# Input rows dealt to partitions in runs, u transposed in 64-row pieces, and held output work given buffers of its own

## The chip, the cores and the metric

One core of a Trainium2 chip runs the kernel. The metric is the device time of one execution in microseconds (us), the median of several runs. Five engines work side by side, each in the order in which its instructions were written: TensorE (PE, matrix multiplication), VectorE (DVE), ScalarE (ACT), GpSimd (POOL) and SyncE (SP). In this kernel SP issues the plain transfers and the transposing transfers, and POOL issues those that change the type on the way from float32 to bfloat16 ("casts"). An instruction that waits for a semaphore holds up everything behind it on its engine.

## The reference: what is computed

There are 8 batches of 3136 rows and 256 columns. The first part is an attention without softmax, the second a gate with a long convolution along the rows, written with FFTs.

```python
scores = (1 / S) * z @ z.T                   # z: S x 64, S = 3136
out    = (np.maximum(scores, 0) ** 2) @ v    # v: S x 256
x      = u * out
proj   = x @ w_proj                          # 256 x 768: x1, x2, x3
x2_conv = irfft(rfft(x2, axis=1) * rfft(filter_fft, axis=0), n=S, axis=1)
y      = (x1 * x2_conv * x3) @ w_out
```

Only the order of the rows inside a batch is free: sums over rows do not depend on it, and the result must stand in the original order in memory.

## The kernel before: how the work is laid out

S is split as 3136 = 64 x 49. A row has the number 49 n1 + n2, with n1 below 64 and n2 below 49. The convolution is a two-step Fourier transform: first over n1 (64 points, `dft1`, one matmul with the table `T1` for two values of n2 at once), then over n2 (49 points, with the tables `S2`). The way back uses `TZ` and `T4`. On chip a tile of 128 partitions holds two values of n2, 64 partitions each; NT = 25 such tiles make a batch, the last one half full. Before the change tile t holds n2 = 2t on the lower half and 2t + 1 on the upper half, so that in the on-chip order the rows stand by n2, and within it by n1.

For each batch b:

- POOL casts z, v and u to bfloat16 (`cast_z`, `load_rows`, `cast_u`). z and u go to scratch in memory, `z16d` and `u16d`, already in the on-chip order: a write of 64 numbers of z, or of 256 numbers of u (512 B), at a time. v goes to SBUF.
- SP reads them back transposed: `ldz` for z (one transfer, `zT`), `load_uT` for u (one transfer for each of seven chunks of 384 to 512 rows, `uT`).
- For each chunk of columns: scores into PSUM (`score_mm`, L1066), ReLU on ACT (L1104), square on ACT or DVE (L1110, L1112) into one of 7 buffers `A`, then v times A (`weigh`, L1135). DVE multiplies with `uT` (L1177) and gives `xT`.
- `add_proj` multiplies xT with w_proj: two parts become the gates (L775, L787, L793), one goes through `dft1` (L821, L653) and is put into scratch memory (`put`, L660).
- `add_spectrum`, when all seven chunks of a batch are in: 8 groups. Each loads its part (`load_spec`, L683), does the second transform (L866), the product with the filter's spectrum (L888), the transform back (L910), and puts the result (`gs_t`, two buffers, L933).
- `add_end`: 7 groups. Each loads (`load_c`, L694), transforms over n1 (L964), multiplies with the gates (L971), multiplies with w_out (L1002), evicts into an output buffer (`ost_t`, two buffers) and stores (L1029).

The order of all instructions is not written by hand. Each piece is a `Task` with a cost on each engine that may do it, the tasks that it depends on and the buffers that it takes. `Plan.go` simulates the engines with these costs when the kernel is built and emits each engine's instructions in the order in which it starts them. PE takes scores (kind S) and v times A (W) first, and fills in the rest (FA, FB, FZ) between them; so the spectrum and the end of batch b run while batch b + 1 does its scores. The planner counts 1.3 us of SP for a `load_uT` and 1.3 for a store.

The last batches are treated apart. Of batch 6 only the first group of `add_end` runs as usual; the other six are held back for the time when batch 7 has no more scores (kind FZ). They depend on `q_`, the last square of batch 7, and load into the buffers `A`, which are free from then on. Their output uses the two `ost_t` buffers. Batch 7's own output uses `R` and `zs` buffers.

At the start POOL issues, in this order: v in two parts with the first part of u between them, two more parts of u, the filter, then the two weight matrices `wp` and `wo` (L346 to L395). The tables are built from `iota` on POOL, DVE arithmetic and a sine on ACT; `percol` (L470 to L479) computes per-partition constants, among them n2 for the row of S2.

Transfers wait on semaphores of which SP and POOL have eight each, taken in turn: a transfer is issued once the one eight before it on the same queue has landed.

Of the kernel before, what the change touches and what calls it, by code (L numbers as in the profile page):

```python
# [11 lines left out]
P = 128  # L12
# [218 lines left out]
def kernel(  # L231
# [27 lines left out]
    z16d = [dram.tile([S, P], BF16, name=f"z16d{i}") for i in range(2)]  # L259
# [81 lines left out]
    def rows_n2(x):  # L341
        return x.rearrange("(n2 n1) d -> n1 n2 d", n1=N1)

    def cast_z(b):
        for k in range(2):
            nc.gpsimd.dma_start(out=rows_n2(z16d[b % 2][:, ds(k * dqk, dqk)]), in_=rows_n1(z[b]))  # L346

    def cast_u(b, lo=0, hi=N2):
        nc.gpsimd.dma_start(out=rows_n2(u16d[b % 2][:, :])[:, lo:hi, :], in_=rows_n1(u[b])[:, lo:hi, :])
# [4 lines left out]
    def load_rows(t, src, t0=0, t1=NT):  # L354
        r = rows_n1(src)
        for j in range(2):
            e = min(t1, (N2 + 1 - j) // 2)
            nc.gpsimd.dma_start(
                out=t[ds(j * N1, N1), t0:e, :], in_=r[:, 2 * t0 + j : 2 * (e - 1) + j + 1 : 2, :]
            )  # L360
# [15 lines left out]
    for i, (t0, t1) in enumerate(((0, 16), (16, NT))):  # L376
        for j in range(2):
            e = min(t1, (N2 + 1 - j) // 2)
            nc.sync.dma_start(
                out=zf[i][ds(j * N1, N1), 0 : e - t0, :], in_=zr[:, 2 * t0 + j : 2 * (e - 1) + j + 1 : 2, :]  # L380
            )
# [5 lines left out]
    cast_u(0, 0, 8)  # L387
    load_rows(v16[0], v[0], 6, NT)
    cast_u(0, 8, 22)
    cast_u(0, 22, N2)  # L390
    load_rows(filt, moe_filter_fft)
    wp16 = const.tile([P, 2, 3 * D], BF16, name="wp16")
    nc.gpsimd.dma_start(out=wp16[:], in_=moe_w_proj.rearrange("(t p) n -> p t n", p=P))
    wo16 = const.tile([P, 2, D], BF16, name="wo16")
# [75 lines left out]
    def percol():  # L470
# [3 lines left out]
        nc.vector.scalar_tensor_tensor(cp, n2p, -2.0, pf, ALU.mult, ALU.add)  # L474
        nc.vector.tensor_scalar(ph0, cp, -float(QUART), float(QUART), ALU.mult, ALU.add)
# [471 lines left out]
    def add_end(b, lasts, gtasks, tg, kind="FB", src=l_p, dsts=(o_p,), late=0):  # L947
        for t0, nt in tg:
# [7 lines left out]
            for dh in range(2):  # L956
# [12 lines left out]
                def ev(dh=dh, t0=t0, w=w, box=box, yb=yb):  # L969
# [4 lines left out]
                    kind, mm, c_pe(*[rows] * nt), [ld, t4_done, *firsts, *(e for _, e in gtasks)],  # L974
# [50 lines left out]
            def store(t0=t0, nt=nt, rows=rows, ob=ob):  # L1025
                r = rows_n1(out[b])
                for j in range(rows // N1):
                    a = 2 * t0 + j
                    nc.sync.dma_start(out=r[:, a : a + 2 * nt - 1 : 2, :], in_=ob["o"][ds(j * N1, N1), 0:nt, :])  # L1029

            s_ = on("SP", store, 1.3, oe, prio=1, moves=0.45 * nt)
            s_.frees.append((o0, 1))


    uT = {}
# [222 lines left out]
```

## Time and profile before

| | us |
|---|---|
| median of 3 runs (lowest to highest) | 1161.12 (1160.87 to 1162.87) |
| the profiled execution | 1163.63 |
| its span, first to last instruction | 1161.9 |
| PE busy | 1112.9 (96%) |
| ACT busy | 1049.2 (90%) |
| DVE busy | 929.6 (80%) |
| POOL busy | 67.5 (6%) |
| chain that ended last: PE, DMA, DVE, ACT | 87%, 5%, 3%, 2% |

How to read what follows. Times in the profile are in us from the start of the span unless a row says ns. A row of a timeline has the start, the length, the engine, the source line and operation, what it writes and reads, and how many instructions were merged. `SPq` is SP's queue: the length of a DMA row is the time for which SP was busy issuing it, not the time until its data landed. A group's row ends with the engine's idle time before its instructions and what ended it (the releaser). A row of waits reads: engine and tile, line, what it waited for, us in total, times, longest. A row of stretches has the stretch, its length, the busy time of PE, PE's weight loads, DVE, ACT and POOL (number of instructions in brackets), the granted share of TensorE's clock, the DMA share and GB/s. Line numbers are those of the kernel before.

### The profile page before, as it was taken

Reading aid. Unit: us, or ns where it says so; the run is one execution under the profiler, and the core shown is the slowest. Engines: PE = TensorE matmul, PEld = TensorE weight load, DVE = VectorE, ACT = ScalarE, POOL = GpSimd, SP = SyncE. Lnnn points to the kernel's source line nnn. Section 1 sums busy time; section 2 is a strip of 40 time slices with the busy share of each in tenths; the row PEclk is TensorE's granted clock in tenths of the full one; section 3 lists DMA queues with packets and bytes.
Section 4 is the critical chain, followed back from the end, with each engine's and each line's share of the span. In section 5 each row is a group of like instructions: output and inputs, shape, how many; then the busy total and the mean of one; then the engine's idle time right before and its main releaser. Section 6 shows DMA issues by size and latency. Waiting matters only on the chain.

```text
span 1161.9 us, 18975 instructions
## 1 busy us (share of the span) xinstructions
PE 1112.9 (96%) x6903; PEld 545.8 (47%) x6903; DVE 929.6 (80%) x1358; ACT 1049.2 (90%) x1464; POOL 67.5 (6%) x80
## 2 busy tenths in 40 slices
PE   5899999999999999899999999999999999999974
PEld 2344445544455444345445543555445454454463
DVE  5898889887798788689788877888778876887673
ACT  5899999999999999798999999998999999999862
POOL 4110002000110002000020001100020000000000
PEclk9999999999999999899999999999999999999987
DMA  9973719443791439934296534944399342312266
GB/s 175 115 115 76 130 56 197 86 121 98 109 197 50 102 78 188 147 91 108 62 186 120 125 89 86 208 97 113 85 118 187 99 111 52 96 49 59 63 191 187
DMA packets 274222, 134.24 MB, mean 116 GB/s; under 512 B 128576, under 2 KB 260800, under 8 KB 274128
## 3 DMA queue, kind: packets, MB, share of 16 engines
q1 hardware_dynamic: 175664, 99.58, 36.2%
q0 software_dynamic: 98464, 33.44, 25.5%
q8 instruction: 54, 0.88, 0.3%
q14 instruction: 40, 0.33, 0.1%
HBM read 94.98 MB, written 71.45 MB: 143 GB/s over the span
## 4 chain that ended last, share of the span: by engine, by line
PE 87%; DMA 5%; DVE 3%; ACT 2%; issue 1%; POOL 1%; SPq 0%; ACTq 0%; DVEq 0%; POOLq 0%
PE ps_o_t L1135 45%; PE ps_s_t L1066 13%; PE ps_m_t L910 4%; PE ps_m_t L821 4%; PE ps_m_t L787 4%; PE ps_m_t L775 4%; PE ps_m_t L1002 3%; DMA wp<-in_moe_w_proj_dram 3%; PE ps_m_t L866 2%; PE ps_m_t L653 2%; PE ps_m_t L964 2%; DMA spec<-gs_t 1%; PE ps_s_t L1068 1%; ACT R_t L1104 1%; PE ps_m_t L735 1%
## 5 line engine op out<-in xcount | busy, mean ns | idle before, releaser
L1135 PE MATMUL ps_o_t<-A_t,v_t 128*128 128x512 bf16 (+4 forms) x2800 | 652.2, 354 | 0.6 <-DVE A_t L1112 0.2
L1104 ACT ACTIVATE R_t<-ps_s_t 128x1024 f32<-128x1024 f32 (+5 forms) x728 | 616.6, 890 | 28.1 <-PE ps_s_t L1066 22.0
L1112 DVE TENSOR_TENSOR A_t<-R_t 128x768 bf16<-128x768 f32 (+3 forms) x411 | 432.8, 1061 | 73.7 <-ACT R_t L1104 50.9
L1135 PEld LDWEIGHTS <-v_t 128*128 128x128 bf16 (+1 forms) x2800 | 255.1, 98 | 242.3 <-issue 84.1
L1110 ACT ACTIVATE A_t<-R_t 128x1024 bf16<-128x1024 f32 (+4 forms) x317 | 288.7, 916 | 21.9 <-PE ps_o_t L1135 17.4
L1066 PE MATMUL ps_s_t<-zT_t 64*128 64x512 bf16 (+2 forms) x1344 | 194.4, 357 | 2.9 <-ACT R_t L1104 2.9
L1066 PEld LDWEIGHTS <-zT_t 64*128 64x128 bf16 x1344 | 42.9, 94 | 124.2 <-issue 121.8
L793 DVE TENSOR_TENSOR gate_t<-ps_m_t,x_t 128x512 bf16<-128x512 f32 (+2 forms) x111 | 66.3, 619 | 22.8 <-PE ps_m_t L787 15.9
L329 DVE CAST x_t<-ps_m_t 128x512 bf16<-128x512 f32 (+4 forms) x112 | 67.4, 613 | 20.5 <-PE ps_m_t L821 15.4
L1177 DVE SCALAR_TENSOR_TENSOR xT_t<-ps_o_t,uT_t 128x512 bf16<-128x512 f32 (+2 forms) x112 | 69.0, 618 | 14.0 <-PE ps_o_t L1135 13.6
L888 DVE TENSOR_TENSOR zs_t<-xs_t,H 98x2048 bf16<-98x2048 bf16 x60 | 73.0, 1217 | 0.7 <-ACT xs_t L325 0.2
L971 DVE TENSOR_TENSOR yT_t<-ps_m_t,gate_t 128x128 bf16<-128x128 f32 (+4 forms) x162 | 62.1, 423 | 13.1 <-PE ps_m_t L964 12.7
L910 PE MATMUL ps_m_t<-zs_t,TZ 98*98 98x256 bf16 x460 | 70.3, 276 | 0.5 <-ACT gs_t L325 0.5
L325 ACT ACTIVATE x_t<-ps_m_t 128x512 bf16<-128x512 f32 (+4 forms) x118 | 61.6, 540 | 9.7 <-PE ps_m_t L775 5.3
L910 PEld LDWEIGHTS <-TZ 98*98 98x98 bf16 x512 | 57.6, 126 | 21.8 <-issue 12.0
L821 PE MATMUL ps_m_t<-wp,xT_t 128*128 128x256 bf16 (+1 forms) x400 | 60.1, 274 | 0.6 <-DVE xT_t L1177 0.5
L775 PE MATMUL ps_m_t<-xT_t,wp 128*128 128x512 bf16 (+2 forms) x220 | 56.7, 362 | 3.0 <-DMA wp<-in_moe_w_proj_dram 3.0
L329 DVE CAST s_t<-ps_m_t 128x512 bf16<-128x512 f32 (+2 forms) x70 | 41.2, 592 | 22.4 <-PE ps_m_t L653 21.7
L787 PE MATMUL ps_m_t<-xT_t,wp 128*128 128x512 bf16 (+2 forms) x222 | 56.4, 356 | 0.0
L1002 PE MATMUL ps_m_t<-wo,yT_t 128*128 128x256 bf16 (+1 forms) x338 | 51.9, 276 | 0.4 <-DVE yT_t L971 0.4
L352 POOL COPY tick<-xT_t 1x1 bf16<-1x1 bf16 x14 | 9.7, 694 | 728.9 <-DVE xT_t L1177 728.9
L866 PE MATMUL ps_m_t<-spec_in_t,S 98*98 98x256 bf16 x232 | 46.4, 283 | 5.3 <-ACT gs_t L325 5.3
(134 smaller groups left out, 754.0 us busy)
## 6 DMA issues: line engine op xcount, KB each, us to landing
out_dram<-ost_t SPq DMA_DIRECT2D x84, 256.0 KB
spec_in_t<-spec SPq DMA_DIRECT2D x64, 196.0 KB
spec<-gs_t SPq DMA_DIRECT2D x60, 196.0 KB
u16d<-in_u_dram POOLq DMA_DIRECT2D x7, 1568.0 KB, 16.6
spec<-s_t SPq DMA_DIRECT2D x80, 128.0 KB
spec_in_t<-spec SPq DMA_DIRECT2D x37, 256.0 KB
v_t<-in_v_dram POOLq DMA_DIRECT2D x7, 800.0 KB, 11.8
z16d<-in_z_dram POOLq DMA_DIRECT2D x14, 392.0 KB, 7.3
```

What stands on the lines that cost most here:

```text
L329: nc.vector.tensor_copy(out_, in_)
L775: nc.tensor.matmul(box["p"][:, :cw], wp16[:, k, ds(nb * P, P)], xt["t"][:, k, :cw], start=(k == 0), stop=(k == 1),)
L787: nc.tensor.matmul(box["p3"][:, :cw], wp16[:, k, ds((4 + nb) * P, P)], xt["t"][:, k, :cw], start=(k == 0), stop=(k == 1),)
L821: nc.tensor.matmul(box["p"][:rows, ds(k_ * D, D)], xt["t"][:, k, ds((i + k_) * P, rows)], wp16[:, k, ds(D, D)], start=(k == 0), stop=(k == 1),
L888: nc.vector.tensor_tensor(xb["z"][:KR], xb["x"][:KR].unsqueeze(2).to_broadcast([KR, 4, 2, D]), H[:KR, ds(qq * 4, 4), :, :], ALU.mult,)
L910: nc.tensor.matmul(box["p"][:KR, ds(i * D, D)], TZ[:KR, k, q, :], xb["z"][:KR, h * 2 + i, k, :], start=(k == 0), stop=(k == 1),)
L1002: nc.tensor.matmul(box["p"][:rows, ds(i * D, D)], yb["y"][:, k, ds((i0 + i) * P, rows)], wo16[:, k, :], start=(k == 0), stop=(k == 1),)
L1066: nc.tensor.matmul(ps[:, i, :cw], zt[h, ds((2 * k + i) * P, P)], zt[h, qs], start=True, stop=True)
L1104: nc.scalar.activation(box["R"][:rows, 0:n, :cw], live[un][:rows, 0:n, :cw], AF.Relu)
L1110: nc.scalar.activation(A[:rows, 0:n, :cw], r, AF.Square)
L1112: nc.vector.tensor_tensor(A[:rows, 0:n, :cw], r, r, ALU.mult)
L1135: nc.tensor.matmul(acc[dh][:, :cw], v16[b][:rows, 2 * k + i, ds(dh * P, P)], A[:rows, i, :cw], start=(k == 0 and i == 0), stop=(last and i ...
```

## The change

Three things change.

Tile t now holds n2 = t on the lower half and n2 = 25 + t on the upper half. So a partition's values lie in consecutive rows of memory: v, the filter and z of batch 0 are read, and the output is stored, in one run per partition instead of every second row. `halves` gives the two halves. The table index n2 per partition (`percol`) is computed for the new order, with four more DVE operations.

`cast_u` writes `u16d` in the natural order of the rows, one long run for each n1. The transposing read `load_uT` then has to pick the rows: one transfer for each 64 rows (all n1 of one n2), 6 to 8 for a chunk, 392 in place of 56. `cast_z` still writes in the on-chip order, in four transfers instead of two. At the start u comes in three smaller-first parts of two transfers each, and `wp` is issued before the second part of u.

The held output work of batch 6 loads into six buffers cut from a buffer of v (`cut_in`), which is free when v of batch 6 has been used, and three of its six output groups use buffers cut from another one (`cut_out`). Its loads wait for `held_w`, the last v times A of batch 6, instead of `q_`; its matmuls wait for `q_` as before (`then`). Its stores wait until SP has issued the last spectrum load of batch 7 (`behind`).

The diff, without its unchanged surroundings:

```diff
-    z16d = [dram.tile([S, P], BF16, name=f"z16d{i}") for i in range(2)]
+    z16d = [dram.tile([NT * P, P], BF16, name=f"z16d{i}") for i in range(2)]
...
-    def rows_n2(x):
-        return x.rearrange("(n2 n1) d -> n1 n2 d", n1=N1)
+    def halves(lo, hi):
+        return [(j, lo, min(hi, NT - j)) for j in range(2) if lo < NT - j]
+
+    def in_turn(x):
+        return x[:, :].rearrange("(t j n1) d -> j n1 t d", j=2, n1=N1)
-            nc.gpsimd.dma_start(out=rows_n2(z16d[b % 2][:, ds(k * dqk, dqk)]), in_=rows_n1(z[b]))
-
-    def cast_u(b, lo=0, hi=N2):
-        nc.gpsimd.dma_start(out=rows_n2(u16d[b % 2][:, :])[:, lo:hi, :], in_=rows_n1(u[b])[:, lo:hi, :])
+            for j, lo, hi in halves(0, NT):
+                nc.gpsimd.dma_start(
+                    out=in_turn(z16d[b % 2])[j, :, lo:hi, ds(k * dqk, dqk)],
+                    in_=rows_n1(z[b])[:, NT * j + lo : NT * j + hi, :],
+                )
+
+    def cast_u(b, t0=0, t1=NT):
+        lines = [(NT * j + lo, NT * j + hi) for j, lo, hi in halves(t0, t1)] if (t0, t1) != (0, NT) else [(0, N2)]
+        for lo, hi in lines:
+            nc.gpsimd.dma_start(
+                out=u16d[b % 2][:, :].rearrange("(n1 n2) d -> n1 (n2 d)", n2=N2)[:, lo * D : hi * D],
+                in_=u[b].rearrange("(n1 n2) d -> n1 (n2 d)", n2=N2)[:, lo * D : hi * D],
+            )
-        for j in range(2):
-            e = min(t1, (N2 + 1 - j) // 2)
-            nc.gpsimd.dma_start(
-                out=t[ds(j * N1, N1), t0:e, :], in_=r[:, 2 * t0 + j : 2 * (e - 1) + j + 1 : 2, :]
-            )
+        for j, lo, hi in halves(t0, t1):
+            nc.gpsimd.dma_start(out=t[ds(j * N1, N1), lo:hi, :], in_=r[:, NT * j + lo : NT * j + hi, :])
...
-        for j in range(2):
-            e = min(t1, (N2 + 1 - j) // 2)
+        for j, lo, hi in halves(t0, t1):
-                out=zf[i][ds(j * N1, N1), 0 : e - t0, :], in_=zr[:, 2 * t0 + j : 2 * (e - 1) + j + 1 : 2, :]
+                out=zf[i][ds(j * N1, N1), 0 : hi - lo, :], in_=zr[:, NT * j + lo : NT * j + hi, :]
-    cast_u(0, 0, 8)
+    cast_u(0, 0, 4)
-    cast_u(0, 8, 22)
-    cast_u(0, 22, N2)
-    load_rows(filt, moe_filter_fft)
+    cast_u(0, 4, 11)
+    cast_u(0, 11, NT)
+    load_rows(filt, moe_filter_fft)
...
+        nc.vector.tensor_scalar(ph0, n2p, 0.5, -0.25, ALU.mult, ALU.add)
+        nc.vector.tensor_scalar(ph0, ph0, RND, RND, ALU.add, ALU.subtract)
+        nc.vector.tensor_scalar(ph0, ph0, -float(N2), None, ALU.mult)
+        nc.vector.scalar_tensor_tensor(n2p, n2p, float(NT), ph0, ALU.mult, ALU.add)
...
-    def add_end(b, lasts, gtasks, tg, kind="FB", src=l_p, dsts=(o_p,), late=0):
+    def add_end(b, lasts, gtasks, tg, kind="FB", src=l_p, dsts=(o_p,), late=0, behind=(), then=()):
...
-                    kind, mm, c_pe(*[rows] * nt), [ld, t4_done, *firsts, *(e for _, e in gtasks)],
+                    kind, mm, c_pe(*[rows] * nt), [ld, t4_done, *firsts, *(e for _, e in gtasks), *then],
...
-                    a = 2 * t0 + j
-                    nc.sync.dma_start(out=r[:, a : a + 2 * nt - 1 : 2, :], in_=ob["o"][ds(j * N1, N1), 0:nt, :])
-
-            s_ = on("SP", store, 1.3, oe, prio=1, moves=0.45 * nt)
+                    a = t0 + NT * j
+                    nc.sync.dma_start(out=r[:, a : a + nt, :], in_=ob["o"][ds(j * N1, N1), 0:nt, :])
+
+            s_ = on("SP", store, 1.3, [*oe, *behind], prio=1, moves=0.45 * nt)
+    class Cut:
+
+
+        def __init__(self, n, shape, dtype):
+            self.slots, self.n, self.shape, self.dtype, self.left = Slots(n), n, shape, dtype, []
+
+        def tile(self, shape, dtype):
+            if not self.left:
+                whole = v_p.tile([P, self.n, *self.shape[1:]], self.dtype)
+                self.left = [whole[:, i] for i in range(self.n)]
+            return self.left.pop(0)
+
+    cut_in, cut_out = Cut(6, [P, 4, D], BF16), Cut(3, [P, 4, D], F32)
-            nc.sync.dma_start_transpose(
-                out=uT[b, c][:, :, : CHUNKS[c]], in_=u16d[b % 2][ds(C0[c], CHUNKS[c]), :]
-            )
+            r = rows_n1(u16d[b % 2][:, :])
+            for o in range(0, CHUNKS[c], N1):
+                t, j = divmod((C0[c] + o) // N1, 2)
+                nc.sync.dma_start_transpose(out=uT[b, c][:, :, ds(o, N1)], in_=r[:, NT * j + t, :])
...
-                        nc.sync.dma_start_transpose(out=zT[b][:, :].unsqueeze(1), in_=z16d[b % 2][:, :])
+                        nc.sync.dma_start_transpose(out=zT[b][:, :].unsqueeze(1), in_=z16d[b % 2][0:S, :])
...
+                        held_w = w_
-                        add_end(b - 1, [*held[0], q_], held[1], ends[1:], "FZ", A_p, (o_p,), 4)
+                        early = [*held[0], held_w]
+                        outs = (o_p, cut_out, cut_out, cut_out, o_p, o_p)
+                        add_end(b - 1, early, held[1], ends[1:], "FZ", cut_in, outs, 4, [(loads[-1], ISSUED)], [q_])
```

## The prediction

> **What bounds the kernel now.** I read the page's busy times first, then the table of stretches, then SP's queue in order of time, then the waits, then the end of the chain.
>
> ```profile
> PE 1112.9 (96%) x6903; PEld 545.8 (47%) x6903; DVE 929.6 (80%) x1358; ACT 1049.2 (90%) x1464; POOL 67.5 (6%) x80
> ```
> ```profile
> 0.00:45.00 45.00, 27.70 (x129) 10.53 (x130) 26.37 (x60) 29.27 (x40) 15.90 (x28) 0.96 1.37 170
> 435.00:575.00 140.00, 134.70 (x836) 66.07 (x835) 112.02 (x162) 121.87 (x166) 7.06 (x7) 0.98 0.73 122
> 575.00:710.00 135.00, 134.94 (x843) 65.66 (x841) 109.91 (x154) 129.38 (x180) 6.53 (x7) 1.00 0.65 120
> 1100.00:1162.00 62.00, 38.30 (x298) 30.18 (x298) 33.18 (x68) 28.66 (x53) 0.00 (x0) 0.79 0.64 183
> ```
> The first figure after the length is PE's busy time. From 45 to 1100 us TensorE is idle for 8 us in all, 5.3 of them between 435 and 575. So the middle can hardly gain, and any new stall there longer than a wait's slack is paid in full. What can be won lies in the first 45 us (17.3 idle) and the last 62 (23.7 idle).
>
> SP's queue around the one long stall, and its DMA transposes by line:
> ```profile
> 461.34 1.25 SPq L1041 DMA_TRANSPOSE uT_t<-u16d  x1
> 463.03 0.31 SPq L933 DMA_DIRECT2D spec<-gs_t  x1
> 463.45 12.79 SPq L1084 DMA_TRANSPOSE zT_t<-z16d  x1
> 476.33 1.50 SPq L660 DMA_DIRECT2D spec<-s_t  x2
> 477.93 2.84 SPq L933 DMA_DIRECT2D spec<-gs_t  x2
> ...
> 507.81 1.24 SPq L1041 DMA_TRANSPOSE uT_t<-u16d  x1
> 512.39 0.33 SPq L933 DMA_DIRECT2D spec<-gs_t  x1
> 514.84 2.58 SPq L694 DMA_DIRECT2D spec_in_t<-spec  x5
> ```
> ```profile
> L1041 SPq DMA_TRANSPOSE uT_t<-u16d x56: 1210/1252/2620, 10.6 to 1049.4; - x56
> ```
> The last line is nanoseconds of issue, least, median and most. Chunks of 384, 448 and 512 rows all sit at 1.21 to 1.25 us, so the price is one per instruction, not one per row.
>
> The waits that the change touches (total, times, longest):
> ```profile
> ACT gs_t L325 <- DMA spec<-gs_t: 6.2, 2, 5.2
> PE ps_m_t L964 <- DMA A_t<-spec: 6.5, 1, 6.5
> PE ps_s_t L866 <- ACT ost_t L325: 3.8, 1, 3.8
> PE ps_m_t L775 <- DMA wp<-in_moe_w_proj_dram: 3.0, 1, 3.0
> ```
> And the chain near the end:
> ```profile
> 1108.47 0.63 SPq L1029
> 1109.16 1.06 SPq L1029
> ...
> 1112.14 5.35 DMA spec_in_t<-spec
> ```
> Here SP was issuing stores of held output (L1029) while the spectrum's loads waited behind them.
>
> The engines' orders of the two built programs are equal on PE, ACT and DVE up to the last 3% of the matmuls, but for four small DVE operations at the start. So up to there only SP, POOL and the transfers act.
>
> **The change part by part.** Sums are made against the profiled execution, 1163.63 us for a span of 1161.9; it lies 2.5 us above the median of the runs, 1161.12.
>
> *u turned 64 rows at a time.* 56 transposes become 392 (49 a batch). Their cost each is not in the trace. From below: were it to go by rows, 64/512 of 1.22 is 0.15 us. From above: 2.04 us, which rows show where stores stand ahead of a transpose in the queue. I take 1.22, as the nearest rows show no dependence on rows. A chunk then holds SP for 9.8, 7.3 or 8.5 us (8, 6 or 7 turns) in place of 1.25. That is 392 x 1.22 - 56 x 1.25 = 408 us more of SP, and no path of its own: uT's readers start 46 to 60 us after it has landed (the first three chunks 16 to 42). What counts is who is queued behind a burst. I walked SP's rows with bursts in place and compared each late row with its slack (landing to the first instruction that waited for it, in the trace's landings):
> - the loads for the last stage (L694), behind the seven turns of the last chunk. At 507.81 the burst ends at 516.3; the put due at 512.39 follows, lands about 2.3 later, and the loads go at 518.9, not 514.84: 4.1 late with 3.1 slack, 1.0 lost. The same reckoning costs 2.0 at 649 (5.0 late, 3.0 slack) and 1.2 at 781 (6.4 and 5.2), and nothing at 237, 379, 916 and 1054. Together 4.
> - the puts of gs_t (L933), two buffers, behind eight turns. At 326 7.0 late with 5.4 slack: 1.6. At 615 4.8 and 3.9: 0.9. Elsewhere the slack holds (203: 3.7 of 5.0; 743: 6.2 of 11.1; 879: 5.7 of 9.4). Together 3 with rounding up for the queue of puts behind.
> - the filter's first load at 115.9, 6.4 late behind the burst of 112.45, slack 0.1; but it took 8.0 to land beside the cast of v, and 2.5 to 2.7 are usual: 1 lost.
> - spectrum puts (L660, slack 12 and more) and stores (late 7.7 at 253, slack 9.3): nothing.
>
> *Casts.* Reads of u, v and the filter and the writes of u become runs of up to 25 KB in place of 512 B. POOL issues two casts of z more per batch (1.39 us each; POOL is 6% busy). The stall at 477.93 comes from a put that took 10.6 us to land, with a transpose of z held for 12.79 us (3.99 at least elsewhere) beside the cast of u. Now the eight turns of 461.34 fill that time and the z transpose starts about 474, when the cast (issued at 462.8; casts of u take 16.6 us to land in the median) is nearly in. I take the 5.3 us of stall as gone: bounds 0 and -8 (TensorE's clock is at half for some us after it).
>
> Sum of the middle: 4 + 3 + 1 - 5 = +3; from -5 (bursts free) to +25 (the rival below).
>
> *Start.* wp moves up the POOL queue, past three casts of u and two of the filter; it lands at 40.9 now, and the 3.0 us wait for it goes. Late next: POOL issues 14 DMAs in place of 11 before the iota of L511 (11.62), and a DMA waits until the one eight before it has landed (L395 waited 1.0 for that). wo's turn then comes when the second large half of v is in, 18.1 now. The iota feeds DVE's L520 (14.99), and the first squares are queued behind it: 4 us late, made good at most where the wait for wp was. The four DVE operations (0.15 each, at 2 us, DVE idle until 7.99) are hidden. Net -0.5; between -3 and +3.
>
> *Tail.* The loads of held output move from 1094.5 to about 1059, into a free buffer of v; stores of held output go behind the last spectrum load. Those loads then leave when the last put has landed (SP's row ends at 1104.85, plus 1.44: 1106.3) and not at 1110.38. They would land at 1109, before L866's start at 1114.30; PE is still in held work until about 1111, so 3 us. Held matmuls among the spectrum's (1.6 us) and the stores between its loads go: 2. The final stores, contiguous, should cost SP 0.33 (as the 2 KB rows of L683, 0.34) and not 0.61 each: of the last five, 4.2 us, 1.5 go. Those held matmuls that move ahead of 1100 move, and add nothing. Put and load before the last stage (6.5 us) stay. Together -7; between -4 and -10.
>
> Sum: +3 - 0.5 - 7 = -4.5: 1159.1 for the profiled execution, 1156.6 for the median. I say 1157.
>
> *A rule against the change.* A turn is now 64 x 256 x 2 = 32 KB. The Trainium skill, "DMA: Bandwidth & Descriptors", Rules for kernel authors, says to merge many small transfers, since below 64 KB overhead is most of what one pays; the same page puts a fixed 2.0 us on a transfer. Estimated by that page, 336 added turns paid one after another are 672 us, not 410. The rows here show SP free after 1.22 while the data land 1.8 later, so turns overlap; the rule's side is the second rival's.
>
> **The rivals.**
> 1. *The casts hold the turns: slower.* SP stays on a transpose while earlier transfers are unfinished: 12.79 at 463.45 against 3.99 elsewhere, 8.8 us. If runs of 25 KB hold the turns as much in each of six batches, the puts of gs_t behind come 8.8 later; less some 4.5 us of slack left, 4 us a batch, 24 in all: 1181, or 1169 if half. It decides from 0.7 us a batch. For: the casts of u and z's transposes meet in every batch. Against: a cast that moves the same bytes in longer runs should not be in flight longer. The Trainium skill, "DMA: Bandwidth & Descriptors", Queues, rings and completion order, says that a DMA engine changes queues only between packets; no row here shows casts with runs that long.
> 2. *A turn costs 2.04.* 0.8 more on 7 or 8 turns puts the last stage's loads 5.7 later and the gs puts 6.5: about 12 a batch, 7 batches, 1240.
> 3. *Turns go by rows (0.15).* Middle -5: 1149.
> 4. *Nothing net.* The bursts eat the tail's gain: 1161. The reading that the change does not do what it says has no ground: the built program has the 392 turns.
>
> **How the numbers follow.** Forecast 0.40, rival 1 0.34, rival 2 0.06, rival 3 0.10, rival 4 0.10. This kernel's runs tell a change from none at about 0.2% (2.3 us). Faster: forecast and rival 3, 0.50; same: 0.10; slower: 0.40. The range leaves out rival 2 and the far ends of 1 and 3: 1147 to 1179. The forecast's own is 1152 to 1159.
>
> **What would show it.** Right: uT transposes x392 at about 1.2 us; no wait for wp at 41 us; L866 after the last batch's loads without an ACT ost_t wait; the last stage's loads landing late by 1 to 2 us in three batches; PE idle in the middle under 12 us. Wrong: waits of gs_t on its puts in every batch, z transposes of 10 us and more, turns over 1.4 us, or a clock below 0.98 in the middle stretches.

## The result: slower, and the profile after

| | us |
|---|---|
| before, median (lowest to highest of 4) | 1161.34 (1160.87 to 1162.87) |
| changed, median (lowest to highest of 4) | 1200.59 (1197.36 to 1206.35) |
| ratio, 95% interval | 1.0341 (1.0293 to 1.0389) |
| span of the profiled execution, before and changed | 1161.9 and 1201.8 |

The forecast was 1157 with a range of 1147 to 1179. The time lies 21.6 us above the range.

Line numbers are now those of the changed kernel: L1161 is v times A, L1069 the turns of u, L945 the put of gs_t, L672 the put of the spectrum's parts, L695 the spectrum's loads, L706 the last stage's loads, L1041 the stores, L878 the second transform, L976 the transform over n1, L787 and L799 the gates. The page's busy times of the changed kernel:

```profile
PE 1128.7 (94%) x6903; PEld 550.9 (46%) x6903; DVE 927.4 (77%) x1357; ACT 1051.5 (87%) x1469; POOL 61.2 (5%) x97
```

TensorE is idle for 73 us of the span, where it was idle for 49, and its busy time is 16 us longer for the same 6903 matmuls. The table of stretches says where (stretch, length, busy PE, PE loads, DVE, ACT, POOL, granted clock, DMA share, GB/s):

```profile
0.00:45.00 45.00, 28.71 (x148) 11.88 (x149) 27.99 (x66) 31.05 (x43) 15.04 (x33) 1.00 0.86 157
45.00:165.00 120.00, 111.87 (x663) 50.95 (x661) 97.60 (x167) 106.11 (x150) 3.90 (x11) 0.94 0.45 92
435.00:575.00 140.00, 132.84 (x823) 65.64 (x821) 111.28 (x163) 117.33 (x160) 6.45 (x9) 0.96 0.56 123
575.00:710.00 135.00, 128.17 (x750) 60.33 (x748) 101.02 (x136) 117.26 (x163) 5.92 (x9) 0.95 0.52 109
1140.00:1202.00 62.00, 43.08 (x336) 31.74 (x332) 32.58 (x66) 35.29 (x65) 0.00 (x0) 0.82 0.60 181
```

The first 45 us hold 19 matmuls more than before and the last 62 us hold 38 more, so both ends gained. The middle lost: 7 or 8 us idle in each of the three stretches shown, where it had been 0 to 5 (45 to 165: 1.9), and a clock of 0.94 to 0.96 where it had been 0.98 to 1.00. The turns, and SP's queue around the time of the old long stall:

```profile
L1069 SPq DMA_TRANSPOSE uT_t<-u16d x392: 1157/1234/4988, 9.3 to 1103.5; - x196
```
```profile
472.12 1.26 SPq L672 DMA_DIRECT2D spec<-s_t  x2
...
482.53 0.31 SPq L945 DMA_DIRECT2D spec<-gs_t  x1
485.75 0.31 SPq L695 DMA_DIRECT2D spec_in_t<-spec  x1
487.10 16.75 SPq L1069 DMA_TRANSPOSE uT_t<-u16d  x8
503.95 0.50 SPq L945 DMA_DIRECT2D spec<-gs_t  x1
504.64 3.66 SPq L1110 DMA_TRANSPOSE zT_t<-z16d  x1
```

A turn takes 1.234 us in the median, 4.988 at most. The transpose of z, 12.79 us before, is down to 3.66, and the eight turns ahead of it now take 16.75 us: two a turn, with the cast of u issued at 483.22 beside them. Some 2.5 us of that SP waits for the spectrum put of 472.12 to land, the transfer eight before its third turn. The put of gs_t stands behind the turns. The waits (in all, times, longest):

```profile
DVE gs_t L329 <- DMA spec<-gs_t: 13.5, 3, 5.8
ACT gs_t L325 <- DMA spec<-gs_t: 13.1, 5, 3.8
PE ps_m_t L976 <- DMA spec_in_t<-spec: 9.7, 6, 4.0
PE ps_m_t L747 <- DMA spec_in_t<-specf: 5.7, 1, 5.7
DVE s_t L329 <- DMA spec<-s_t: 6.6, 2, 4.4
```

Waits of gs_t on its puts were 6.2 us, on ACT alone; they are now 26.6 for both engines. The waits for the last stage's loads in the middle and for the filter's loads are new; the wait for the put of a spectrum part was 0.2 us. The waits for `wp` at 41 us and of L866 for ACT's ost_t are gone. The chain in the changed kernel's middle holds late landings of transfers that SP had issued in good time:

```profile
196.00 9.91 DMA spec<-gs_t
...
472.12 23.13 DMA spec<-s_t
495.27 1.16 SPq L1069
...
503.95 3.35 DMA spec<-gs_t
```
```profile
625.23 8.57 DMA spec<-gs_t
684.08 2.46 DMA spec<-gs_t
```

A put of gs_t takes some 2.5 us to land as a rule (2.46 and 2.74 in these rows and the next). The three transfers of 8.57 to 23.13 us were issued 3 to 10 us after POOL had issued a cast of v (at 186.06, 468.73 and 615.24).

And the tail, in the changed kernel's chain:

```profile
1176.38 2.74 DMA spec<-gs_t
1179.24 3.08 DMA A_t<-spec
1182.37 0.62 PE ps_m_t L976 x4
```

**Where the 40 us came from.** PE, ACT and DVE have the same order in both kernels but for four small DVE operations at the start, up to 1100 us of the kernel before: for 6596 of 6903 matmuls, so up to the last 4% and not 3%, as the prediction had it. So the start of the k-th weight load in one trace less that in the other tells how late the one is at that point. In the changed kernel this shift goes from -2.4 us at 46 us of the kernel before to +47.4 at 1075, and the end is 39.9 later: the tail gained 7.5. The steps in between come at a dozen places. The table sets them beside what the prediction's walk along SP's queue had put there, and beside three of the experiments below, whose PE order is the same.

| at (us, kernel before) | what is late | predicted | changed | turns only | turns, u in on-chip order, long v | the same, short v |
|---|---|---|---|---|---|---|
| 73-78 | put of a spectrum part | 0 | 4.7 | 0.8 | 0 | 0 |
| 124 | filter's first load | 1 | 6.8 | 6.8 | 7.9 | 7.2 |
| 195 | put of gs_t | 0 | 4.9 | 0 | 0 | 0 |
| 338 | put of gs_t | 1.6 | 6.7 | 5.5 | 8.2 | 4.5 |
| 465-484 | spectrum put, put of gs_t | 0 | 10.8 | 0 | 1.2 | 0.2 |
| 489-495 | old stall gone | -5 | -8.1 | -6.4 | -6.1 | -7.5 |
| 521 | last stage's loads | 1.0 | 1.3 | 1.6 | 1.2 | 1.1 |
| 607 | put of gs_t | 0.9 | 5.8 | 0 | 4.2 | 0 |
| 655 | last stage's loads | 2.0 | 6.7 | 7.3 | 7.2 | 5.9 |
| 789 | last stage's loads | 1.2 | 5.7 | 2.9 | 2.9 | 3.1 |
| 877-957 | puts, stores | 0 | 3.0 | 3.2 | 4.6 | 2.2 |
| 1063 | last stage's loads | 0 | 1.6 | 1.7 | 1.4 | 1.4 |

The first of these places in the changed kernel (SP's queue, waits between 66 and 90 us, and the stretch that follows):

```profile
59.98 9.38 SPq L1069 DMA_TRANSPOSE uT_t<-u16d  x5
69.46 1.00 SPq L672 DMA_DIRECT2D spec<-s_t  x2
```
```profile
DVE s_t L329 <- DMA spec<-s_t: 2.2, 1, 2.2
PE ps_o_t L1161 <- ACT A_t L1136: 1.6, 1, 1.6
```
```profile
73.96:80.79 6.83, 6.58 (x25) 2.06 (x25) 4.56 (x9) 5.32 (x9) 0.16 (x2) 0.50 0.49 123
```

Five turns beside the cast of u (issued at 56.05) hold SP for 9.38 us, and the puts of a spectrum part go at 69.46 instead of 66.19. DVE waits 2.2 us for one of them and ACT 1.4, TensorE then waits for ACT, and its clock is at half for the next 6.8 us. The kernel before already waited 0.2 us for this put, so it had no slack.

### The profile page after: what moved, and what is told of

Its sections match the earlier page's. It is cut to its first block, busy times and chain, and to the rows that moved or that the text cites. A ratio compares the mean times of both kernels' runs of the same rounds, so it can differ in the third digit from the quotient of the medians.

```text
span 1201.8 us, 19421 instructions
## 1 busy us (share of the span) xinstructions
PE 1128.7 (94%) x6903; PEld 550.9 (46%) x6903; DVE 927.4 (77%) x1357; ACT 1051.5 (87%) x1469; POOL 61.2 (5%) x97
## 4 chain that ended last, share of the span: by engine, by line
PE 77%; DMA 10%; ACT 4%; DVE 4%; SPq 2%; issue 2%; POOL 0%; ACTq 0%; DVEq 0%; POOLq 0%
PE ps_o_t L1161 40%; PE ps_s_t L1092 11%; DMA spec<-gs_t 4%; PE ps_m_t L799 3%; PE ps_m_t L787 3%; PE ps_m_t L833 3%; PE ps_m_t L1014 3%; PE ps_m_t L922 3%; ACT R_t L1130 3%; SPq L1069 2%; DMA spec<-s_t 2%; PE ps_m_t L665 2%; PE ps_m_t L878 2%; PE ps_m_t L976 2%; DMA spec_in_t<-spec 1%
## 5 line engine op out<-in xcount | busy, mean ns | idle before, releaser
L1161 PE MATMUL ps_o_t<-A_t,v_t 128*128 128x512 bf16 (+4 forms) x2800 | 663.4, 359 | 6.3 <-DVE A_t L1138 4.4
L1161 PEld LDWEIGHTS <-v_t 128*128 128x128 bf16 (+1 forms) x2800 | 257.6, 98 | 254.3 <-issue 98.4
L983 DVE TENSOR_TENSOR yT_t<-ps_m_t,gate_t 128x128 bf16<-128x128 f32 (+3 forms) x169 | 64.8, 425 | 33.9 <-PE ps_m_t L976 33.7
L787 PE MATMUL ps_m_t<-xT_t,wp 128*128 128x512 bf16 (+2 forms) x222 | 56.6, 359 | 2.8 <-DVE gs_t L329 2.8
L799 PE MATMUL ps_m_t<-xT_t,wp 128*128 128x512 bf16 (+2 forms) x220 | 56.1, 358 | 3.1 <-ACT gs_t L325 3.1
L878 PE MATMUL ps_m_t<-spec_in_t,S 98*98 98x256 bf16 x238 | 48.1, 285 | 7.9 <-DVE gs_t L329 7.9
L325 ACT ACTIVATE gs_t<-ps_m_t 98x512 bf16<-98x512 f32 x68 | 41.0, 606 | 16.2 <-DMA spec<-gs_t 13.1
## 6 DMA issues: line engine op xcount, KB each, us to landing
u16d<-in_u_dram POOLq DMA_DIRECT2D x7, 1568.0 KB, 11.6
```

The costliest lines, as they stand in the source:

```text
L325: nc.scalar.activation(out_, in_, AF.Copy)
L787: nc.tensor.matmul(box["p"][:, :cw], wp16[:, k, ds(nb * P, P)], xt["t"][:, k, :cw], start=(k == 0), stop=(k == 1),)
L799: nc.tensor.matmul(box["p3"][:, :cw], wp16[:, k, ds((4 + nb) * P, P)], xt["t"][:, k, :cw], start=(k == 0), stop=(k == 1),)
L1161: nc.tensor.matmul(acc[dh][:, :cw], v16[b][:rows, 2 * k + i, ds(dh * P, P)], A[:rows, i, :cw], start=(k == 0 and i == 0), stop=(last and i ...
```

## The experiments

All ratios are to the kernel before on the same chip; a difference of 0.01 is 11.6 us.

| kernel | median us | ratio (95%) |
|---|---|---|
| e1: changed, one transpose per chunk | 1149.79 | 0.9919 (0.9888 to 0.9949) |
| e2: before, with turns | 1182.99 | 1.0204 (1.0172 to 1.0237) |
| e3: changed, u cast row by row across n1 | 1262.10 | 1.0898 (1.0857 to 1.0939) |
| e4: before, with held output's buffers | 1156.35 | 0.9971 (0.9949 to 0.9992) |
| e5: e1 with turns | 1190.63 | 1.0300 (1.0254 to 1.0346) |
| e6: changed, u cast every other row | 1191.70 | 1.0286 (1.0255 to 1.0318) |
| e7: changed, planner knows the burst's cost | 1181.05 | 1.0217 (1.0170 to 1.0264) |
| e8: e1 with an early iota | 1145.03 | 0.9888 (0.9860 to 0.9916) |
| e10: e5 with v and the filter every other row | 1180.53 | 1.0186 (1.0150 to 1.0222) |
| e11: e5 with turns planned singly | 1165.37 | 1.0052 (1.0029 to 1.0076) |
| e12: e8 with v every other row | 1144.31 | 0.9888 (0.9854 to 0.9921) |
| e13: changed, turns planned singly | 1175.51 | 1.0175 (1.0103 to 1.0246) |
| e14: e11 with v every other row | 1149.27 | 0.9917 (0.9887 to 0.9947) |

### Which part loses: u's new cast and its turns (e1, e2)

e1 puts u's cast back into the on-chip order, and with it one transpose per chunk (the diff is cut to its main lines; `u16d` also gets room for the full 25 tiles, and the loop runs over `halves`).

```diff
-                out=u16d[b % 2][:, :].rearrange("(n1 n2) d -> n1 (n2 d)", n2=N2)[:, lo * D : hi * D],
-                in_=u[b].rearrange("(n1 n2) d -> n1 (n2 d)", n2=N2)[:, lo * D : hi * D],
+                out=in_turn(u16d[b % 2])[j, :, lo:hi, :],
+                in_=rows_n1(u[b])[:, NT * j + lo : NT * j + hi, :],
...
-            for o in range(0, CHUNKS[c], N1):
-                t, j = divmod((C0[c] + o) // N1, 2)
-                nc.sync.dma_start_transpose(out=uT[b, c][:, :, ds(o, N1)], in_=r[:, NT * j + t, :])
+            nc.sync.dma_start_transpose(
+                out=uT[b, c][:, :, : CHUNKS[c]], in_=u16d[b % 2][ds(C0[c], CHUNKS[c]), :]
+            )
```

> The changed kernel with the cast of u written in the on-chip order again (runs of 512 B on the writing side, two transfers) and one transpose for each chunk, 56 in all; the split of the rows, the reads of v and z in long runs, the contiguous stores, the start's order and the held output's buffers stay. Theory A (the bursts of 64-row turns, lengthened by the long runs of the cast of u, make the 47 us that the changed kernel loses ahead of the last stage): the loss goes and the tail's 7 us stay, so 1150 to 1158 us, SP's transposes at 1.25 us each. Rival V (the long runs of the cast of v hold the puts by themselves): the late landings beside the casts of v at 124, 195 and 604 us stay, some 15 to 25 us of the loss with them, 1170 to 1180 us.

Measured: 1149.79. The whole loss lies in these two edits, and without them the change gains 9 us by the ratio. Theory A and rival V were about who makes the loss; V is out as a cause by itself, but comes back below in another form.

e2 adds nothing but the turns to the kernel before:

```diff
-            nc.sync.dma_start_transpose(
-                out=uT[b, c][:, :, : CHUNKS[c]], in_=u16d[b % 2][ds(C0[c], CHUNKS[c]), :]
-            )
+            for o in range(0, CHUNKS[c], N1):
+                nc.sync.dma_start_transpose(
+                    out=uT[b, c][:, :, ds(o, N1)], in_=u16d[b % 2][ds(C0[c] + o, N1), :]
+                )
```

> The kernel before with nothing changed but the reading of u: 392 transposes of 64 rows in place of 56, from the same rows in the same order, all casts in their short runs. Rival B (the number of turns alone costs the time, through SP's 408 us): 1190 us or more. Theory A (long runs of casts hold the turns): bursts of 8 take 9.8 to 10.5 us also beside the casts, and the queue's lateness by the walk of the prediction costs 8 us or less, so 1161 to 1172 us.

Measured: 1182.99, between the two. Turns in bursts cost 24 us by the ratio with all casts in short runs, so theory A, which gave them 8 or less, is too narrow, and rival B's 1190 is not reached either. One place shows why the price is so much above the walk. SP's queue in e2, where the prediction had 2.0 us at 649, and the table of stretches around it:

```profile
648.93 10.29 SPq L1042 DMA_TRANSPOSE uT_t<-u16d  x7
659.32 0.51 SPq L933 DMA_DIRECT2D spec<-gs_t  x1
661.82 2.58 SPq L694 DMA_DIRECT2D spec_in_t<-spec  x5
```
```profile
640.00:660.00 20.00, 19.89 (x122) 10.02 (x121) 16.75 (x22) 19.29 (x24) 0.00 (x0) 1.00 0.17 46
660.00:672.00 12.00, 7.36 (x41) 3.64 (x41) 4.66 (x8) 4.85 (x8) 0.00 (x0) 0.72 0.56 164
663.42:670.25 6.83, 5.48 (x27) 2.60 (x27) 3.04 (x6) 2.13 (x3) 0.00 (x0) 0.50 0.87 252
672.00:700.00 28.00, 27.70 (x196) 14.09 (x195) 22.84 (x40) 25.78 (x38) 0.00 (x0) 1.00 0.47 116
```

The seven turns take 10.29 us and not the 8.5 that were reckoned; the put and the loads behind it move on as one chain, and TensorE stands for 4.6 us. Its clock is 0.72 over the 12 us around the stall, and half from 663.42 to 670.25. The shift at this place is 7.3, so some 2.7 of it is put down to the clock.

### Turns and runs told apart (e5, e6, e3, e10, e12)

e5 is e1 with the turns of e2 (the same diff, on e1).

> The changed kernel with the cast of u in the on-chip order (runs of 512 B) but with the 392 turns of 64 rows, now from consecutive rows; against the changed kernel only the natural-order cast of u is undone, against the kernel with one transpose per chunk (1149.8 us) only the turns are added. Theory C (turns and the natural cast each cost about half): the turns cost here what they cost alone, 22 us, so 1168 to 1176 us, and the remaining 25 to 32 us to the changed kernel belong to the natural cast. Rival A (nearly all from the natural cast holding the bursts): 1158 to 1165 us. Rival B (the turns alone, together with the long runs of v that this kernel keeps): 1190 us or more.

Measured: 1190.63, rival B's number: turns cost 41 us in this structure against 22 to 24 in the kernel before. From e5 to the changed kernel there are 10 us by the medians, 5 by the ratios, whose intervals overlap; for bursts the natural-order cast of u is not resolved from none by these two. In e6 u is cast in natural order, but in two transfers of every other row, so that a run is one row.

```diff
...
-                out=u16d[b % 2][:, :].rearrange("(n1 n2) d -> n1 (n2 d)", n2=N2)[:, lo * D : hi * D],
-                in_=u[b].rearrange("(n1 n2) d -> n1 (n2 d)", n2=N2)[:, lo * D : hi * D],
+            for k in range(2):
...
+                    out=rows_n1(u16d[b % 2][:, :])[:, lo + k : hi : 2, :],
+                    in_=rows_n1(u[b])[:, lo + k : hi : 2, :],
```

> The changed kernel with the natural-order cast of u in two transfers, even and odd rows, so that a run is one row (512 B written, 1 KB read) and the walk through memory stays that of the changed kernel, n1 outermost; the turns stay. If the length of the runs makes the natural cast dear: the bursts beside it return to 10-11.5 us and the time to that of turns with an on-chip-order cast, some 1170 us (1165 to 1178). If it is the place of the rows (a turn reads 64 rows 25 KB apart, however they were written): 1195 to 1206 us as the changed kernel.

Measured: 1191.70, the time of e5 to within its spread: where the 64 rows of a turn lie makes no difference that the runs resolve. Both expectations on the time failed, since each took the turns for cheaper or the runs for dearer than they are. The trace holds what was expected of the bursts: beside the cast of u at 484 us eight turns take 11.0 us (two rows of SP's queue together), where the changed kernel took 16.75, the step of 10.8 us at 465 to 484 is 0.4, and the one at 73 to 78 is gone, as in e5. The steps at 195 and 607 are there in e6 too (4.5 and 2.8), so u's long runs are not needed for them. By the shifts the middle costs 31.8 us in e6, 33.3 in e5 and 49.8 in the changed kernel, so there u's long runs cost some 16; the medians (10) and the ratios (5) give less, and e6 starts 5 us later, with twice as many transfers of u.

e3 was the first try at short runs of u, with n2 in the outer loop:

```diff
-                out=u16d[b % 2][:, :].rearrange("(n1 n2) d -> n1 (n2 d)", n2=N2)[:, lo * D : hi * D],
-                in_=u[b].rearrange("(n1 n2) d -> n1 (n2 d)", n2=N2)[:, lo * D : hi * D],
+                out=u16d[b % 2][:, :].rearrange("(n1 n2) d -> n2 n1 d", n2=N2)[lo:hi, :, :],
+                in_=u[b].rearrange("(n1 n2) d -> n2 n1 d", n2=N2)[lo:hi, :, :],
```

> The changed kernel with the cast of u cut into runs of 512 B (1 KB on the reading side), the same bytes to the same places in natural order; the 392 turns stay and so do the long runs of v. Theory A: the bursts of 8 beside the casts of u return from 14.3-16.8 us to about 10.5, and half or more of the 47 us goes: 1165 to 1182 us. Rival B (turns alone): no difference over 5 us, 1195 to 1206 us.

Measured: 1262.10, which no theory had. The same pieces of 512 B as in e6, but each 25 KB from the one before it, make the cast itself slow, and the waits on puts grow with it. The page's DMA issues and waits of e3:

```profile
u16d<-in_u_dram POOLq DMA_DIRECT2D x7, 1568.0 KB, 29.7
```
```profile
ACT gs_t L325 <- DMA spec<-gs_t: 43.6, 8, 8.5
DVE gs_t L329 <- DMA spec<-gs_t: 34.8, 5, 11.4
```

So e3 changed two things, and says nothing on the length of runs alone; e6 does.

The runs of v are left. e10 is e5 with v and the filter read every other row (`lo + k : hi : 2` on both sides, k = 0 and 1), in twice as many transfers.

> The kernel with turns from an on-chip-order u (1190.6 us), with v and the filter read every other row (runs of 1 KB in memory, 512 B in SBUF) in twice as many transfers. If the long runs of v are why the turns cost 41 us here and 22 us in the kernel before: 1172 to 1180 us. If v's runs do not matter: 1188 to 1195 us (the four more transfers at the start can cost up to 3).

Measured: 1180.53. The ratio falls by 0.0114 from e5's, with intervals apart. In the table of steps 607 is gone and 338 halved, and that although the six added transfers at the start cost 4 us there. e12 asks whether long runs of v cost anything by themselves; it has one transpose per chunk.

> The kernel with one transpose per chunk and the early iota (1145.0 us, 0.9888 of before), with v of batches 1 to 7 read every other row in twice as many transfers, as in the kernel with turns where that gained 10 us. If v's long runs cost time only where 64-row turns stand beside them: no change, a ratio to before of 0.986 to 0.992. If they cost by themselves: 5 to 10 us less, a ratio of 0.980 to 0.984.

Measured: a ratio of 0.9888, the same as without the edit. In these kernels long runs of v cost something only where turns stand beside them.

### What a turn costs by itself: the order on SP (e7, e13, e11, e14)

The planner counted 1.3 us of SP for what takes 7.6 to 10. e7 tells it the cost of a burst and changes nothing else in the program's text; the order of all engines is planned anew.

```diff
-        t = after(on("SP", go, 1.3, deps, [uT_p.slots], moves=2.0), at)
+        t = after(on("SP", go, 1.25 * CHUNKS[c] / N1, deps, [uT_p.slots], moves=2.0), at)
```

> The changed kernel in which the planner counts 1.25 us for each turn (10 us for a burst of eight) in place of 1.3 us for all of them; the instructions are the same, their order is planned anew on all engines. If the loss is one of order (puts and loads planned into times in which SP is still in a burst): a third or more of the 40 us goes, 1165 to 1188 us. If SP's bursts and the landings beside the casts cost it whatever the order: 1192 to 1206 us.

Measured: 1181.05, half of the loss gone by the medians, 14 us by the ratios. The next step makes each turn a task of its own, below all else that SP may issue, so that puts and loads go between two turns:

```diff
...
+            k = on(
+                "SP", go, 1.25, [(prev, ISSUED)] if prev else deps, [] if prev else [uT_p.slots], prio=2,
+                moves=2.0 * N1 / CHUNKS[c],
+            )
...
```

e9 and e13 are this edit on the changed kernel. Three executions of e9 lay between 1173.83 and 1192.65, and the profiled one took 2994.45: there a matmul of v times A took 808 ns in the mean, against 359 in the changed kernel, though the granted clock on record is 1.00. So e9 decides nothing and was measured again as e13.

> The changed kernel with its long-run cast and its 392 turns, but each turn is a task of its own for the planner, of 1.25 us and with lower priority than puts, loads and stores, so that these may go between two turns of a burst. If the loss is what waits on SP behind an undivided burst (puts of gs_t, loads for the last stage, the filter's first load): most of what knowing the cost of whole bursts left goes too, 1158 to 1172 us. If turns and landings beside the casts cost time wherever they stand: no better than with whole bursts of known cost, 1178 to 1190 us.

> The changed kernel with each of its 392 turns planned singly, the long-run cast kept (the same kernel as the one whose executions disagreed). If what waits behind a burst is most of the loss here too: 1165 to 1180 us, that is 20 to 35 us under the changed kernel's 1200.6. If the long runs of u hold single turns as they hold bursts: 1181 to 1192 us.

Measured for e13: 1175.51, 25 us under the changed kernel, though the interval is wide (1.0103 to 1.0246). Then the same edit where u is cast in the on-chip order, with long and with short runs of v:

> The kernel with turns from an on-chip-order u (1190.6 us), its turns planned singly at 1.25 us and below all else on SP. If standing behind a burst is the whole price of the turns: the time of one transpose per chunk, 1149.8 us, to 1156 us. If the occupation of the DMA engines and the late landings are a part of it: 1165 to 1180 us.

> The kernel with turns from an on-chip-order u, planned singly (1165.4 us), with v of batches 1 to 7 read every other row. If the rest of the turns' price is v's long runs holding them: 1150 to 1158 us. If it is the turns themselves wherever they stand: 1161 to 1168 us.

Measured: 1165.37 and 1149.27. e14 has all 392 turns and the time of e1, which has 56 transposes (0.9917 and 0.9919, each within 0.003; by e12 the runs of v make no difference to the latter's kind). So planned singly, and with u and v in short runs, 336 more turns cost nothing that the runs resolve. What costs is, in this structure, 25 us by the medians (29 by the ratios) for undivided bursts that the planner took for 1.3 us (e5 to e11), and 16 us for v's long runs beside singly planned turns (e11 to e14). The 25 us belong to the new plan as a whole: TensorE's own order differs from e5's from 124 us on, and no run changes SP's order alone. With u's long runs as well, singly planned turns cost 10 us more by the medians, 14 by the ratios (e11 to e13; 1.0052 and 1.0175, intervals apart).

How the runs do it is seen at one place that all three have: the turns beside the casts of v and u that POOL issues between 310 and 337 us. SP's queue in e13 (u and v in long runs), e11 (v alone) and e14 (neither):

```profile
332.79 27.53 SPq L1071 DMA_TRANSPOSE uT_t<-u16d  x6
360.67 3.40 SPq L1118 DMA_TRANSPOSE zT_t<-z16d  x1
```
```profile
333.47 13.65 SPq L1068 DMA_TRANSPOSE uT_t<-u16d  x6
347.31 5.87 SPq L1117 DMA_TRANSPOSE zT_t<-z16d  x1
```
```profile
325.79 8.50 SPq L1071 DMA_TRANSPOSE uT_t<-u16d  x6
334.47 9.04 SPq L1120 DMA_TRANSPOSE zT_t<-z16d  x1
```

Six turns hold SP for 27.53, 13.65 and 8.50 us, while the casts move 4.01 MB in each: in 6576, 9664 and 12704 packets, by the traces' counts. In e13 this one place stops TensorE for 12.8 us, in e11 for 5.2, and in e14 no wait of TensorE stands there:

```profile
ACT gs_t L325 <- DMA spec<-gs_t: 14.8, 2, 13.1
PE ps_m_t L787 <- ACT gs_t L325: 12.8, 1, 12.8
```

(Waits of e13 between 325 and 366 us: TensorE's gate matmul waits for an eviction on ACT, which waits for the put of gs_t that has not landed.) The puts that are waited for stand in the chains of e13 and of e11:

```profile
332.44 27.92 DMA spec<-gs_t
```
```profile
328.26 11.40 DMA spec<-gs_t
```

SP had issued both ahead of the six turns. So at this place the put does not stand behind the turns; it is in flight beside them and the casts, and lands after 27.92 and 11.40 us. Of the 27.53 us of e13, 6.1 are SP's own wait for puts of a spectrum part to land.

### The two ends (e4, e8)

e4 is the kernel before with `Cut`, `behind`, `then`, `held_w` and `outs` of the diff, and no other part.

> The kernel before with the held output's part of the change alone: buffers cut from two buffers of v, loads from the last v times A of batch 6, stores behind the last spectrum load. If the tail's part of the prediction holds, 4 to 7 us faster than before (the stores keep their 0.61 us, so the 1.5 us of the prediction's 7 are not in it): 1154 to 1157 us. If the spectrum's start is bound by PE in the held matmuls in any case: 1160 to 1162 us.

Measured: 1156.35 and a ratio of 0.9971 (0.9949 to 0.9992): a gain of 3.4 us by the ratio. In the profiled executions the span is 8.2 shorter, 2.7 of it before the tail (the old stall, 2.88 us instead of 5.30; nothing near it was changed, so I take it for chance), 5.5 in the tail.

e8 is e1 with T1's iota and memset ahead of the second part of u's cast on POOL.

> The kernel with one transpose per chunk (1149.8 us) and one edit at the start: POOL makes the index table of the first transform (iota and memset) ahead of the second part of the cast of u, not after all first transfers. If the late iota costs what the shift against the kernel before shows (TensorE 3 us late at 25 us, made good at 41 where the wait for the first weights was): 2 to 4 us less, 1146 to 1148 us. If the start is bound by something else, such as the landing of v's second part: no change, 1149 to 1151 us.

Measured: 1145.03. The intervals of e1 and e8 overlap, but the traces agree with the medians: TensorE is 5.2 us earlier at 20 us, 6 at 46 and 3.7 at the end of the middle. POOL's rows of the changed kernel and of e8:

```profile
13.05 0.51 POOL L369 DMA_DIRECT2D v_t<-in_moe_filter_fft_dram  x1 [2.38 <-DMA v_t<-in_v_dram]
15.88 0.73 POOL L403 DMA_DIRECT2D wo<-in_moe_w_out_dram  x1 [2.31 <-DMA v_t<-in_v_dram]
16.62 0.28 POOL L523 IOTA kcol<- 128x128 int32 x1
```
```profile
5.01 0.75 POOL L397 DMA_DIRECT2D wp<-in_moe_w_proj_dram  x1
5.74 0.31 POOL L399 IOTA kcol<- 128x128 int32 x1
```

e8 is the best version found, with e12 level: 1.1% under the kernel before (0.9860 to 0.9916).

## Why the prediction was wrong, step by step

The step that failed is the sum of the middle. It was put at +3 us (4 + 3 + 1 - 5) and measured +49.8 (from -2.4 to +47.4 in the shift), while the start and the tail came as forecast. Two of its terms were wrong: the walk along SP's queue, which priced the bursts at 8 us where undivided bursts in this order cost 25 (e5 to e11), and the casts' long runs, priced at nothing but the vanished stall, where v's cost 16 us (e11 to e14) and u's 5 to 16.

- **The bound** (TensorE full in the middle, new stalls paid in full): right, and it was an understatement. A stall is paid more than in full, since the clock is at half for some us around its end and after it (0.50 over 6.83 us at two places above). In the changed kernel TensorE's busy time grew by 16 us with no matmul added.
- **A turn costs 1.22 us of SP**: right in the median, 1.234. Rival 2 (2.04) and rival 3 (0.15) fall. Against that row the prediction had set a rule of the Trainium skill, "DMA: Bandwidth & Descriptors", Rules for kernel authors: merge transfers, as below 64 KB one pays mostly overhead. SP's rows agree with it: 1.2 us an instruction, with 64 rows as with 512. The estimate by that page, 672 us of turns one after another (its fixed 2.0 us is a fit to transfers issued from GpSimd), is not what happened: six turns in a row hold SP for 8.50 us in e14, and e14 pays nothing that the runs resolve for 336 more transfers of 32 KB.
- **The walk of slacks (4 + 3 + 1 us)**: this step failed in size. Its places were right: filter, puts at 338, loads at 521, 655 and 789 all appear with turns alone. They measured 24 us there (e2: 6.8 + 5.5 + 1.6 + 7.3 + 2.9) against 6.8 for the same five, and places with a reckoned price of nothing gave 5 more (877 to 1063); the sixth place, the put at 607, cost nothing in e2. Puts of a spectrum part were put at nothing, for a slack of 12 us and more, but the one at 73 us had none and cost 4.7 in the changed kernel. Missing were the length of real bursts (10.29 for 7 turns, first turn of a burst 2.4 us), what follows a late put in the same chain, and the clock after a stall. The walk also took the order on SP as given. That the planner made this order with 1.3 us a burst was written in the part before the prediction; that a new plan was then worth 25 us was not drawn from it.
- **Casts: "a cast that moves the same bytes in longer runs should not be in flight longer"**: true and beside the point. The cast of u landed sooner (median 11.6 us, before 16.6), but what is in flight beside it came later: turns of 2 us and more, puts of 8.57 to 23.13. Rival 1 had the mechanism and about half of the loss, 24 us, at a chance of 0.34; it looked for it behind the transposes of z, which became shorter (2.98 to 5.94 us), and at the casts of u alone. The casts of v do it too: 16 us in e11 to e14. For rival 1 the prediction had cited the Trainium skill, "DMA: Bandwidth & Descriptors", Queues, rings and completion order, by which a DMA engine changes queues only between packets. No run here watches an engine do so; the three bursts above, longer the fewer packets the same bytes come in, agree with it.
- **The old stall (-5)**: it went, and brought 8.1: the 5.3 us of stall and the slow clock after it. It went in e1 too (-8.0), without a turn, so the turns that were to fill the time are not what removed it. In e4 it was half as long (-3.4), where nothing near it was changed, so part of it is likely chance; one trace of each is all there is.
- **Start (-0.5; -3 to +3)**: -2.4 at 46 us, inside the bounds. The wait for `wp` went, and the iota came late, as said; e8 shows that the lateness was worth 4 to 6 us (3.6 by the ratios, 6 in the trace at 46 us) and could be avoided.
- **Tail (-7; -4 to -10)**: -7.5, right (the terms 3, 2 and 1.5 make 6.5, which the prediction wrote as 7). The spectrum's loads left at 1154.02, 1.4 us after the last put's row, and L878 began at 1158.06 behind held matmuls with no wait. Of the parts, 3.6 lie before L878, 2.3 between it and the last stage's loads, and some 1.5 from there to the end. The last of these came for another reason than the one given: the final stores were to cost SP 0.33 us each and not 0.61, but the last 13 measured 0.73 and 0.72 in the median by their two buffers, where the kernel before had 0.62 and 0.68.
- **The signs named for "wrong"**: waits of gs_t on its puts, a clock below 0.98 and single turns over 1.4 us all came; z transposes of 10 us did not.

What stays open: how much u's long runs cost with undivided bursts (5 by the ratios, 10 by the medians, 16 by the shifts); how much of the 25 us SP's order alone is worth; and by what means the casts in long runs hold the transfers beside them, which the three bursts suggest and nothing shows.

## What to carry to other kernels

When one instruction on a queue becomes eight, ask first what the planner or the hand that ordered the queue believes it costs: here 392 turns were free once each was a task of its own beside short runs, and cost 25 us more as 56 lumps counted at 1.3 us. Merging a cast into long runs made the cast of u land sooner here, and the turns and puts beside the casts land later, so lengthen runs with care where something short and urgent is in flight at the same time (v's long runs: no price without turns, 10 to 16 us with them). Price a stall on TensorE above its length: here 4.6 us of stall cost 7.3.

## What was not expected of the hardware

- A transpose of u holds SP for 1.2 us in the median with 64 rows as with 512, so its price is one per instruction; eight in a row take some 11 us (11.00 in e6), 16.75 beside a cast in long runs.
- A plain put of a spectrum part landed 23.13 us after its issue in the changed kernel, and a put of gs_t after 27.92 in e13, with casts of v and u in long runs and turns under way; 2.5 us is usual for a put of gs_t.
- Casting the same rows in the same 512 B pieces took 29.7 us in the median with n2 outermost (e3); with n1 outermost two halves, issued together at 484 us, were in after 10.2 and 14.5 us (e6). The kernel was 70 us slower for it.
- A stall of 4.6 us came with a clock of 0.72 over 12 us, the stall included, and of one half over 6.83 of them (e2).
